# Recurrent memory attention: the chain reduced to its 8 memory rows, x attention in tiles of three segments between its steps

## Chip, cores, metric

One core of one Trainium2 chip. The metric is the time of one execution in device microseconds (us), median of several runs. In the profiles PE is the matrix engine, DVE, ACT and POOL are VectorE, ScalarE and GpSimd, and SP is SyncE, which issues loads and stores; SBUF is the on-chip memory, PSUM that of matmul results.

## The reference, cut to what matters

64 segments of 32 rows of x, one after the other. Each attends over 8 memory rows and its own 32 rows; the 8 memory rows of its output are the memory of the next segment. The kernel computes the output and all gradients (one forward, one backward recurrence). Around it stand a layer norm and a gated feed-forward, which the change hardly touches.

```python
M, seg, H, Dh, Dm = 8, 32, 32, 128, 640      # S = 2048 rows
mem = mem0
for s in range(n_seg):                        # 64 segments
    h = concatenate([mem, xs[s]])             # 40 rows
    q, k, v = (einsum('btd,dhe->bhte', h, W) for W in (Wq, Wk, Wv))
    scores = where(mask, einsum('bhqe,bhke->bhqk', q, k) * scale, -1e9)
    o = einsum('bhqk,bhke->bhqe', softmax(scores), v)
    o = einsum('bhte,hed->btd', o, Wo)
    mem = o[:, :M]                            # the recurrence
    outs.append(o[:, M:])
# result: x + attention * silu(feed_forward(xn)), then the vjp of it all
```

## The kernel before, where the change works

One forward step projects all 40 columns of a segment with the weights as the stationary operand, 128 of them at a time, and adds the x attention of the segment before (`x_attention`, 32 rows by 40) in the same step. The weights stay in SBUF.

```python
def f1_group(hT, qT, kT, h0, nh):
    for (W_, dstp, ceng) in ((Wq, qT, 's'), (Wk_, kT, 'v')):
        pj = ps.tile([P, 12, L], F32, name="pj", tag="pj")          # L = 40
        for hh in range(nh):                                         # hidx = h0 + hh
            for dc in range(DC):                                     # DC = 5
                nc.tensor.matmul(pj[:, hh, :], W_[:, dc, hidx * P:(hidx + 1) * P], hT[:, dc, :], ...)
        k.copy(dstp[:, h0:h0 + nh, :], pj[:, 0:nh, :], eng=ceng)
...
for step in range(T + 1):
    t, tp = step, step - 1
    if t < T:
        ...                                   # load x columns
        v_build(t, hT, vtile)                 # V of memory rows, column-tiled by 4
        for (h0, nh) in hgroups:
            f1_group(hT, qT, kT, h0, nh)      # Q and K of 40 columns
        mem_attention(t, qT, kT, vtile)
    if tp >= 0:
        x_attention(tp, qTs[tp % 2], kTs[tp % 2], vts[tp % 2])
    ...
    for dc in range(DC):                      # output product of 40 columns
        for jc in range(H):
            nc.tensor.matmul(pso[:, dc, :], Wo[:, jc, dc * P:(dc + 1) * P], oTc[:, jc, :], ...)
    ...                                       # next memory, stores
```

The backward recurrence is built the same way (gradients of Q, K, V of 40 rows, three products with transposed weights of 128 columns). The weight gradients follow in a dense stage of their own.

## Time and profile before

| | before |
|---|---|
| median of all runs | 6478.06 us (4 runs, 6474.34 to 6487.07) |
| PE busy | 85% of the span |
| forward recurrence | 1636 us, 25.2 us a step |
| backward recurrence | 2197 us, 34.3 us a step |
| attention weight gradients | 1185 us |

The table by stage and the groups stand in the prediction. The page of the profile cuts the span in 40 slices: the digit is PE's busy share in tenths, and under it the granted clock of PE in tenths of full speed.

```profile
PE   6869999999999579999999999997457878888777
...
PEclk9888888888888679899989899888668989999888
```

In the two recurrences (slices 4 to 13 and 16 to 27) PE is at 9 and the clock mostly at 8 to 9. Over the whole loops it is 0.82 and 0.90.

### The profile page before, as it was taken

The page shows a single profiled execution, that of the slowest core. Times are in us where ns is not written, and L with a number is a line of the kernel's source. Part 1 is how long each engine was busy: PE and PEld are TensorE (multiplying, and loading weights), DVE is VectorE, ACT ScalarE, POOL GpSimd, SP SyncE. Part 2 cuts the span into 40 slices and gives each one's busy share as a digit, 9 for nine tenths or more (in the row PEclk, how much of TensorE's full clock was granted, in tenths as well). Part 3 has the DMA queues.
Part 4 walks back from the last instruction along what each step waited for, and adds up shares of the span by engine and source line. Part 5 has one row for each costly group of instructions (what it writes and reads, how often), then busy time and mean ns, then how long its engine had stood idle before and what let it go on. Part 6 is the DMA issues. An engine that isn't in the chain of part 4 may idle for free.

```text
span 6475.0 us, 255034 instructions
## 1 busy us (share of the span) xinstructions
PE 5517.9 (85%) x117287; PEld 4293.8 (66%) x117490; DVE 2584.9 (40%) x5438; ACT 1820.3 (28%) x3535; POOL 348.9 (5%) x783
## 2 busy tenths in 40 slices
PE   6869999999999579999999999997457878888777
PEld 3426888888888478888888888887123444444344
DVE  5414555555555433344334334333237422222212
ACT  3313444444333222222222222222112022222212
POOL 0000010110011000000000000000000001111110
PEclk9888888888888679899989899888668989999888
DMA  5363333333322652222223223224757655545674
GB/s 178 128 218 101 87 93 91 96 93 89 83 72 70 198 177 83 82 89 84 89 83 90 80 85 89 83 82 79 179 180 192 161 155 196 191 155 171 222 255 165
DMA packets 844915, 824.64 MB, mean 127 GB/s; under 512 B 466240, under 2 KB 652608, under 8 KB 839232
## 3 DMA queue, kind: packets, MB, share of 16 engines
q10 hardware_dynamic: 485568, 399.76, 21.0%
q1 hardware_dynamic: 354496, 387.58, 19.0%
q8 instruction: 918, 15.04, 1.0%
q0 software_dynamic: 3776, 20.97, 0.9%
q14 instruction: 157, 1.29, 0.1%
HBM read 516.86 MB, written 291.22 MB: 125 GB/s over the span
## 4 chain that ended last, share of the span: by engine, by line
PE 65%; DMA 17%; DVE 10%; issue 4%; ACT 3%; ACTq 0%; POOL 0%; another core or an unknown queue 0%; DVEq 0%; SPq 0%; POOLq 0%
PE pgh L949 13%; PE pj L589 6%; PE gacc L1310 5%; PE pso L717 5%; PE pgo L871 4%; PE pgxb L1111 2%; DMA hb_tok<-HB 2%; PE oacc L1336 2%; PE pgot L925 2%; DMA fullxx<-OT 2%; PE pvx L545 2%; PE ptokk L917 2%; PE ptokq L917 1%; PE pv L600 1%; DMA fullx<-GQT 1%
## 5 line engine op out<-in xcount | busy, mean ns | idle before, releaser
L1310 PE MATMUL gacc<-gtok_all,h_all 128*128 128x512 bf16 x2322 | 559.5, 390 | 45.9 <-DVE gwo L92 20.6
L1310 PEld LDWEIGHTS <-h_all 128*128 128x128 bf16 x2400 | 237.1, 100 | 321.2 <-issue 81.5
L949 PE MATMUL pgh<-gQT,WqT 128*128 128x40 bf16 x10240 | 351.1, 183 | 12.7 <-issue 6.3
L949 PE MATMUL pgh<-gKT,WkT 128*128 128x40 bf16 x10240 | 334.6, 182 | 21.8 <-DMA WkT<-WKT 15.7
L717 PE MATMUL pso<-oTc,Wo 128*128 128x40 bf16 x10400 | 344.4, 197 | 5.2 <-issue 1.4
L94 ACT COPY qtok<-ptokq 40x1024 bf16<-40x1024 bf16 x128 | 128.8, 1006 | 768.4 <-PE ptokq L917 768.4
L717 PEld LDWEIGHTS <-Wo 128*128 128x128 bf16 x10400 | 338.8, 108 | 8.2 <-issue 2.6
L949 PE MATMUL pgh<-gVT,WvT 128*128 128x40 bf16 x10240 | 322.0, 182 | 8.9 <-issue 7.9
L949 PEld LDWEIGHTS <-WqT 128*128 128x128 bf16 x10240 | 308.9, 98 | 22.4 <-issue 8.6
L954 DVE CAST goT<-pgh 128x40 bf16<-128x40 f32 x63 | 12.6, 200 | 775.3 <-PE pgh L949 762.1
L949 PEld LDWEIGHTS <-WkT 128*128 128x128 bf16 x10240 | 297.7, 97 | 27.4 <-DMA WkT<-WKT 15.8
L589 PEld LDWEIGHTS <-Wq 128*128 128x128 bf16 x10240 | 275.8, 96 | 46.2 <-issue 45.9
L1279 PE MATMUL pt<-ident,xsrc 128*128 128x128 bf16 x2048 | 172.8, 247 | 152.7 <-DVE xsrc L1268 74.0
L589 PE MATMUL pj<-hT,Wq 128*128 128x40 bf16 x10240 | 290.8, 180 | 14.2 <-ACT qT L94 14.1
L949 PEld LDWEIGHTS <-WvT 128*128 128x128 bf16 x10240 | 292.0, 97 | 11.7 <-issue 10.3
L871 PE MATMUL pgo<-goT,WoT 128*128 128x40 bf16 x10240 | 277.9, 180 | 25.2 <-DMA WoT<-WOT 15.7
L589 PE MATMUL pj<-hT,Wk 128*128 128x40 bf16 x10240 | 290.6, 180 | 2.5 <-issue 2.2
L871 PEld LDWEIGHTS <-WoT 128*128 128x128 bf16 x10240 | 268.1, 96 | 35.1 <-DMA WoT<-WOT 15.8
L1279 PEld LDWEIGHTS <-xsrc 128*128 128x128 bf16 x2048 | 151.1, 112 | 208.9 <-issue 97.5
L589 PEld LDWEIGHTS <-Wk 128*128 128x128 bf16 x10240 | 273.4, 96 | 3.5 <-issue 3.5
L671 POOL TENSOR_TENSOR Px<-ex,rz 32x480 bf16<-32x480 bf16 (+1 forms) x192 | 171.3, 892 | 1460.2 <-DVE rz L670 1125.8
L1271 POOL COPY msrc<-fullx 128x128 bf16<-128x128 bf16 x512 | 152.9, 318 | 1762.3 <-DMA fullx<-GQT 991.0
(255 smaller groups left out, 9652.1 us busy)
## 6 DMA issues: line engine op xcount, KB each, us to landing
fullx<-OT SPq DMA_DIRECT2D x128, 320.0 KB
fullxx<-OT ACTq DMA_DIRECT2D x128, 320.0 KB
fullx<-GQT SPq DMA_DIRECT2D x64, 320.0 KB
fullx<-GQT ACTq DMA_DIRECT2D x64, 320.0 KB
fullx<-GKT SPq DMA_DIRECT2D x64, 320.0 KB
fullx<-GKT ACTq DMA_DIRECT2D x64, 320.0 KB
fullx<-GVT SPq DMA_DIRECT2D x64, 320.0 KB
fullx<-GVT ACTq DMA_DIRECT2D x64, 320.0 KB
```

What stands on the lines that cost most here:

```text
L545: nc.tensor.matmul(pvx[:, :], xnTt[:, dc, :], Wv[:, dc, jn * 512:(jn + 1) * 512], start=(dc == 0), stop=(dc == DC - 1))
L589: nc.tensor.matmul(pj[:, hh, :], W_[:, dc, hidx * P:(hidx + 1) * P], hT[:, dc, :], start=(dc == 0), stop=(dc == DC - 1))
L671: nc.gpsimd.tensor_tensor(Px[:, h0:h0 + nh, :], exv, bc_last(rz[:, 0:nh], L), ALU.mult)
L717: nc.tensor.matmul(pso[:, dc, :], Wo[:, jc, dc * P:(dc + 1) * P], oTc[:, jc, :], start=(jc == 0), stop=(jc == H - 1))
L871: nc.tensor.matmul(pj[:, hh, :], WoT[:, dc, hidx * P:(hidx + 1) * P], goT[:, dc, :], start=(dc == 0), stop=(dc == DC - 1))
L917: nc.tensor.transpose(ptk[:, hh, :], src[:, b8 + hh, :], k.ident[:, :])
L925: nc.tensor.transpose(ptk[:, hh, :], gOT[:, hs + b8 + hh, :], k.ident[:, :])
L949: nc.tensor.matmul(pso[:, dc, :], WT_[:, jc, dc * P:(dc + 1) * P], gX[:, jc, :], start=(i_acc == 0), stop=(i_acc == n_acc - 1))
L1111: nc.tensor.matmul(pgx[:, d0:d0 + dsz], gTt[0:fsz, fc, :], wT[0:fsz, fc, d0:d0 + dsz], start=(i_acc == 0), stop=(i_acc == n_acc - 1))
L1271: nc.gpsimd.tensor_copy(msrc[:, mt2, :, r4, j * M:(j + 1) * M], fulls[j][:, hs:hs + H2, 0:M])
L1279: nc.tensor.transpose(pt8[0:nrow, hh, :], xsrc[:, b8 + hh, 0:nblk, :], k.ident[:])
L1310: nc.tensor.matmul(accs[dc][:, :], h_all[:, kt, dc * P:(dc + 1) * P], gtok[:, kt, jn * 512:(jn + 1) * 512], start=(kt == 0), stop=(kt == N ...
```

## The change

The intent: of the 40 rows of a segment only the 8 memory rows are in the chain from segment to segment. So the chain keeps those alone. Q, K and V of x rows come from dense products ahead of the loop (672 rows) or ride in 24 spare columns of the chain's projection. The projection takes the 32 columns as the stationary operand, in four column tiles of the array at once, and streams the weights. x attention of three segments (24 memory and 96 x rows, a mask between segments) is done in units of 4 heads, as filler between the chain's steps. What one stage hands to another goes through memory. The diff, cut to its core:

```diff
-        def f1_group(hT, qT, kT, h0, nh):
-            ...
-                        nc.tensor.matmul(pj[:, hh, :], W_[:, dc, hidx * P:(hidx + 1) * P], hT[:, dc, :],
+def packed_proj(k, ps, tag, x, W, st, cp):
+    for b in range(2):
+        pj = ps.tile([P, 512], F32, name="pj", tag=tag)
+        for dc in range(k.DC):
+            for g in range(4):
+                c0 = g * 1024 + b * 512
+                nc.tensor.matmul(pj[32 * g:32 * g + 32, :], x[:, dc, :], W[:, dc, c0:c0 + 512],
+                                 ..., tile_position=(0, 32 * g), skip_group_check=True)
+        k.copy(st[:, b * 512:(b + 1) * 512], pj[:], eng=cp[b])
...
-        for step in range(T + 1):
-            ...
+            def xattn(tl, qd):                        # one filler unit: 4 heads of a tile
+                ...                                   # row loads of Q and V on nc.sync
+                pt = ps.tile([P, 4, n], BF16, name="qpt", tag="xt", bufs=1)
+                ...                                   # transposes, copy, mask and scores
+                for j in range(4):
+                    nc.scalar.activation(E[0:n, j, :], sp[:, j, :], ACT.Exp, ...)
+                nc.gpsimd.tensor_tensor(Pb[0:n], E[0:n], bc_last(rz[0:n], n), ALU.mult)
+                nc.gpsimd.dma_start(k.PR[tl][:, h0:h0 + 4, :], Pb[0:n])
+                pp = ps.tile([n, 4, n], BF16, name="xpp", tag="xt", bufs=1)
+                ...                                   # transposes of P, values, store
+            for tl in range(k.NTL + 1):
+                units = []
+                for qd in range(8):
+                    if 0 <= tl - 1:
+                        units.append((xattn, tl - 1, qd))
+                    if tl + 1 < k.NTL:
+                        units.append((kprep, tl + 1, qd))
+                steps = list(range(3 * tl, min(3 * tl + 3, T)))
+                for i, t in enumerate(steps):
+                    with tc.high_priority():
+                        chain(t)
+                    ...                               # a third of the units after each step
...
+    # backward chain: the output gradient goes to memory and comes back by heads
+                nc.sync.dma_start(k.GOS[t].rearrange("r (g c) -> g r c", g=4), sg[:])
+                for a in range(2):
+                    nc.sync.dma_start(gOst[:, a, :], k.GOS[t, 0:8, ...])
...
+    # x gradient, now dense, in the stage of the weight gradients
+                        nc.tensor.matmul(g5[0:nx, :], gT[:, i, j, 0:nx], Ws[i][:, j, 0:512], start=f, stop=l)
+                        nc.tensor.matmul(g1[0:nx, :], gT[:, i, j, 0:nx], Ws[i][:, j, 512:640], start=f, stop=l)
```

## The prediction

> **What bounds the kernel now.** I read first a table of stretches, cut where the first and last instruction of each stage's tiles stand: layer norm and feed-forward forward (to 336), weights and value projection (to 544), the forward recurrence (to 2180), its epilogue, the backward recurrence (2306 to 4503), the feed-forward backward (to 5290), the attention weight gradients.
>
> ```profile
> core 0: us, PE busy (x) PEld busy (x) DVE busy (x) ACT busy (x) POOL busy (x), PEclk, DMA share, GB/s
> 0.00:336.00 336.00, 244.76 (x1499) 131.26 (x1522) 154.61 (x372) 116.92 (x194) 0.84 (x7) 0.91 0.44 151
> 336.00:544.00 208.00, 147.71 (x679) 65.08 (x692) 51.85 (x83) 38.61 (x66) 3.93 (x4) 0.85 0.58 198
> 544.00:2180.00 1636.00, 1560.20 (x46576) 1382.83 (x46572) 892.09 (x1987) 659.02 (x1604) 171.34 (x193) 0.82 0.30 85
> 2180.00:2306.00 126.00, 47.59 (x662) 38.44 (x663) 49.61 (x106) 21.98 (x33) 6.28 (x5) 0.57 1.01 328
> 2306.00:4503.00 2197.00, 2057.47 (x58896) 1911.47 (x58892) 853.35 (x1573) 578.62 (x1006) 13.63 (x63) 0.90 0.29 86
> 4503.00:5290.00 787.00, 516.45 (x2832) 243.27 (x2883) 311.39 (x707) 113.49 (x220) 0.00 (x0) 0.79 0.66 162
> 5290.00:6475.00 1185.00, 943.70 (x6157) 521.46 (x6269) 271.98 (x612) 291.67 (x412) 152.88 (x512) 0.89 0.57 199
> ```
>
> The two recurrences are 3833 of 6475 us, with the PE busy 95% and 94% of them: 25.2 us a step forward (65 steps) and 34.3 us backward (64). They are rows of small matmuls, as the groups say:
>
> ```profile
> L1310 PE MATMUL gacc<-gtok_all,h_all 128*128 128x512 bf16 x2322 | 559.5, 390 | 45.9 <-DVE gwo L92 20.6 <-ACT gtok_all L94 10.7 <-DVE gtok_all L92 5.2
> L949 PE MATMUL pgh<-gQT,WqT 128*128 128x40 bf16 x10240 | 351.1, 183 | 12.7 <-issue 6.3 <-DMA WqT<-WQT 0.5
> L717 PE MATMUL pso<-oTc,Wo 128*128 128x40 bf16 x10400 | 344.4, 197 | 5.2 <-issue 1.4 <-ACT oTc L94 0.5
> ...
> L600 PE MATMUL pv<-Wv,hT 128*8 128x512 bf16 x2560 | 172.7, 383 | 4.4 <-DMA hT<-in_A_mem_dram 4.4
> ```
>
> The mean of one (183 ns) is latency. The pace is start to start in the trace: 25 ns for a 40-column matmul with its own 128-column weights, 56 ns at 128 columns, 216 ns at 512. The pv group is column-tiled in four: its starts come four within 12 ns, then 206 ns later the next four, so four matmuls of 512 cost 216 ns. Full weights thus cost the old kernel almost nothing at 25 ns.
>
> **What the Trainium skill says.** "TensorEngine Tiling (Array Packing)", Performance Considerations, gives each matmul about 60 cycles, so that small ones don't get cheaper; the trace agrees with 25 ns at 8, 32 and 40 columns alike. "TensorE: Matmul & The Clock Gate", Weight-path perf modes, gives fast weight load only to exactly 128 weights; its LDWEIGHTS section has a plain load take columns/1.2 ns. The trace is quicker: 18 ns for 40 columns (Pm), 28 for 64, so columns/2.4; a 120-column weight is then 50 ns, an estimate, against 25 now. The same page, Part 1, says that an idle PE falls to half clock; here the grant is 0.57 in the epilogue and 0.9 in the dense stages. "DMA: Bandwidth & Descriptors", SWDGE vs HWDGE, has GpSimd write the descriptors of its own DMAs; the only four here took 1.03 to 1.72 us of POOL each, and the change issues some 1340 there.
>
> **The change, part by part.** The forward recurrence keeps only the 8 memory rows in its chain; 672 of the x rows are projected densely beforehand, the others ride in 24 spare columns. x attention works in tiles of three segments as filler between chain steps. Gradients of x rows leave the recurrence for a dense stage.
>
> *Before the loop.* 720 matmuls of 512 x 216 ns = 156, 640 transposes at some 75 ns = 48, weights 30: 235 us (now 208). The feed-forward forward takes the 80 transposes of the epilogue: 348.
>
> *One forward chain step*, serially, with about 0.1 us at each handover: Q, K, V as 120 tiled matmuls, 30 x 216 = 6.5, last latency and eviction 1.2; selection 0.35 and copy 0.45; 32 scores on 120-column weights 1.9; copy 0.5, transposes 0.3, maximum and scale 0.7, two exponentials 1.2 (285 to 302 ns for 40 columns now), reciprocal and product 0.65, transposes 0.4, copy 0.45; 32 matmuls on V 1.05; copy 0.45; output, 16 x 136 ns (320 columns) = 2.2 + 0.25; eviction 0.55; six fp32 matmuls, none in this trace, taken at the 0.3 us of the slowest transposes, 1.8; copy 0.25. Sum 21, with filler in the queues 22. So the step falls only from 25.2 to 22: the old projections at 25 ns were good already.
>
> *The filler.* One x-attention unit (4 heads, 8 units per tile of 3 steps) is serial too: scores 0.4, maximum 0.7, scale 0.2, four exponentials 1.7, reciprocal 0.3, POOL product 1.1 (0.98 now), transposes 0.5, copy 0.5, values 0.3, the next unit's K transposes and copy 0.95, Q transposes and copy 1.15: 7.9 us. One PSUM buffer holds both transposes and the K ones, so units don't overlap. The order of the built program shows where they stand: two of three steps have about 1.3 units each, but the first step of a tile has four whole units and a part between Q's selection and its scores, since its K must be ready and the PE runs in order. That is 3.5 + 3 x 7.9 + 6.5 = 34, of which 2 were there anyway: 22 + 32 = 54, or 52 as the filler then is gone. A tile is 2 x 22 + 52 = 96; 21 tiles 2016, the last step 52, a tail of 15 units at 7 = 105: 2173 us, against 1636.
>
> *Output projection*, now its own stage: per tile 32 x (216 + 56 + 42) = 10 us, 22 tiles 220, load 20: 240, against 76.
>
> *Backward.* Weights 35, dense projection of 704 rows 240 x 216 = 52: 87 (now 50). The chain step: projection 10 x 216 with latency and eviction 3.2, selection and copy 0.85, 32 products 1.85, copy and transposes 0.8, softmax gradient 1.2, transposes and copy 0.85, Q gradient 1.5, output 48 x 136 ns = 6.5 + 0.2, eviction 0.55, fold and copy 2: 19.5. Here the order spreads the filler evenly, 2.7 units a step; DVE waits for it add about 1.5: 21. 62 x 21 = 1302, the first steps, which hold some 14 serial units of 5.4, 118: 1420 us, against 2197. A gain of 780.
>
> *Attention weight gradients.* The dense part is new. Per tile and 4 heads: transposes 16 x 54 ns, row gradients 12 x 56 ns, gradient of x 12 x (216 + 56): 4.8 us PE; 8 x 21.5 such are 825, at the 0.8 that the present stage reaches (2400 x 216 + 2560 x 56 ns = 660 of 822 us) 1030. Weight gradients 2640 x 216 = 570 + 30. Output weights 704 x 272 ns = 191, at 0.8 240. Start 10: 1880 us, against 1185.
>
> *Feed-forward backward* loses 80 transposes: 775.
>
> Sum: 348 + 235 + 2173 + 240 + 87 + 1420 + 1880 + 775 = 7158, taken as 7150 us. PE work alone grows: x rows' attention, which lay under the recurrence's weights, is paid again in dense stages.
>
> **Rivals.** (1) The forward filler overlaps after all: if the first step of a tile costs 30 rather than 52, the loop is 1750 and the whole 6700; if also the dense stages run at full pace, 6350. For it: somebody tuned this order; ACT and DVE are at 54% and 40% of the present forward loop. Against: PE order is fixed, and one PSUM buffer ties units together. (2) Faster: chain steps of 18 us both ways and no filler stall give 1300 and 1250 and some 6100. For it: the waits in the backward loop are short now, and the new step has a third of the matmuls. Against: the sums above. (3) Slower: POOL becomes the bound backward, 13 DMAs a step at 1.0 to 1.7 us being 14 to 22 us; or the clock falls to 0.6 in the long filler stretches, where the PE works some 15% of the time: 150 to 300 us, to 7450.
>
> **Range and chances.** Rival 1 and the clock set the range: 6350 to 7700. My sum says slower by 10%, and it takes two errors of its larger terms to come under 6350; but a rebuild of this care is made to win, which I weigh. Faster 0.22, within 2% 0.08, slower 0.70.
>
> **What would show it.** Right: forward steps in a pattern of 22, 22, 52 us; the exponentials and POOL product of x attention on the chain of waits; granted clock under 0.8 forward; about 21 us a step backward; a gradient stage near 1900 us. Wrong: equal forward steps under 25 us; a backward step over 26 with the PE waiting for POOL; a dense stage under 1600.

## The result, and the profile after

| | before | after |
|---|---|---|
| median | 6478.06 us (6474.34 to 6487.07, 4 runs) | 8379.07 us (8372.95 to 8388.02, 4 runs) |
| PE busy | 85% | 72% |
| mean granted clock | 0.86 | 0.79 |

The ratio is 1.294 (95% interval 1.292 to 1.296). Ratios are the mean time of one kernel's fast runs over that of the other's of the same rounds, so not quite the ratio of the medians above. The change makes the kernel slower by 29%; the prediction said 10%.

The stages of after, cut as in the table of before (columns: span, busy time and instructions of each engine, granted clock, DMA share, GB/s):

```profile
core 0: us, PE busy (x) PEld busy (x) DVE busy (x) ACT busy (x) POOL busy (x), PEclk, DMA share, GB/s
0.00:345.00 345.00, 251.25 (x1578) 136.21 (x1602) 161.84 (x393) 125.73 (x210) 3.63 (x25) 0.91 0.54 172
345.00:584.00 239.00, 196.37 (x1360) 129.24 (x1360) 80.87 (x139) 82.76 (x140) 0.00 (x0) 0.90 0.70 246
584.00:3086.00 2502.00, 1630.64 (x21542) 1023.59 (x21543) 642.96 (x1654) 658.02 (x2338) 435.41 (x650) 0.68 0.27 75
3086.00:3313.00 227.00, 226.37 (x2112) 157.39 (x2111) 53.71 (x129) 46.13 (x66) 0.51 (x1) 0.99 0.44 120
3313.00:3415.00 102.00, 58.63 (x240) 25.58 (x244) 18.06 (x29) 13.82 (x24) 0.67 (x3) 0.82 0.77 268
3415.00:5460.00 2045.00, 1397.49 (x24256) 959.06 (x24252) 628.85 (x3184) 315.56 (x784) 675.02 (x1112) 0.71 0.40 109
5460.00:7435.00 1975.00, 1576.96 (x11832) 966.58 (x11832) 484.30 (x1110) 308.72 (x602) 15.76 (x22) 0.94 0.27 76
7435.00:7650.00 215.00, 197.06 (x1408) 107.78 (x1408) 21.19 (x32) 9.49 (x33) 0.00 (x0) 0.95 0.62 133
7650.00:8371.00 721.00, 516.24 (x2739) 240.12 (x2792) 297.86 (x690) 111.90 (x219) 0.00 (x0) 0.80 0.60 165
```

Rows 1 and 2 are the layer norm with the feed-forward and the dense projections; row 3 is the forward loop, row 6 the backward loop, rows 7 and 8 the attention weight gradients. PE is busy 65% of the forward loop and 68% of the backward one, at a clock of 0.68 and 0.71, where the old loops had 95% and 94% at 0.82 and 0.90. The slices of the page show the same:

```profile
PE   7687666666666648576666777758888888787588
...
PEclk9796676666667769776666677789999999997699
```

| stage, us | predicted | measured | difference |
|---|---|---|---|
| layer norm, feed-forward forward | 348 | 345 | -3 |
| weights, dense projections | 235 | 239 | +4 |
| forward loop | 2173 | 2502 | +329 |
| output projection | 240 | 227 | -13 |
| backward weights, dense projection | 87 | 102 | +15 |
| backward loop | 1420 | 2045 | +625 |
| attention weight gradients | 1880 | 2190 | +310 |
| feed-forward backward | 775 | 721 | -54 |
| sum | 7158 | 8371 | +1213 |

So three stages hold the whole miss. What PE waited for in the forward loop (time in total, how often, the longest):

```profile
PE xpp L510 <- POOL xP L506: 378.2, 136, 31.0
...
PE xsp L492 <- ACT qT L486: 77.9, 134, 0.7
PE xpo L515 <- DMA vr<-VS: 77.5, 12, 7.8
...
PE xpo L515 <- DMA vr<-VX: 36.9, 7, 6.8
```

The POOL product of x attention leads, and ahead of it lies a unit's whole softmax; V rows that land late come next. The starts of the first value product of successive chain steps, taken from the trace, are this far apart:

```
us: ... 24.8 24.2 63.0 24.8 24.3 63.8 24.8 24.2 64.6 24.7 24.1 63.3 ...   (predicted 22 22 52)
```

One filler unit inside a 64 us step (start, duration, engine, what, and in brackets the idle time before and who ended it):

```profile
2263.49 0.65 PE L510 MATMUL xpp<-ident,xP 120*120 120x120 bf16 x4 [3.95 <-POOL xP L506]
...
2264.65 0.68 PE L515 MATMUL xpo<-vr,xPT 120*120 120x128 bf16 x4 [0.50 <-DVE xPT L512]
...
2266.10 0.56 PE L484 MATMUL qpt<-ident,qr 120*128 120x120 bf16 x4
...
2267.36 0.66 PE L492 MATMUL xsp<-kT,qT 128*120 128x120 bf16 x4 [0.70 <-ACT qT L486]
...
2270.93 0.98 POOL L506 TENSOR_TENSOR xP<-xE,xrz 120x480 bf16<-120x480 bf16 x1 [4.15 <-issue]
2271.96 0.47 PEld L510 LDWEIGHTS <-xP 120*120 120x120 bf16 x4 [4.13 <-POOL xP L506]
2271.97 0.66 PE L510 MATMUL xpp<-ident,xP 120*120 120x120 bf16 x4 [3.95 <-POOL xP L506]
```

From one `xpp` to the next are 8.48 us, of which PE works some 3.3. Between the scores (2267.36) and the next transposes of P (2271.97) it stands still. The scores of the next unit, which could fill that time, come after those transposes in PE's program. The trace's clock records say that the grant alternates between full and half in stretches of multiples of 3.4 us; in such a 64 us step it is at half for 47.8 us on end, and for 65% of the whole loop.

In the backward loop PE waited for loads:

```profile
PE gvpt L751 <- DMA gvr<-VS: 143.2, 53, 6.8
PE psd L682 <- DMA vTt<-VTD: 130.4, 21, 7.9
PE gkp L775 <- DMA gqx<-QS: 62.6, 16, 7.9
```

These are V rows of the filler, the transposed V of a tile (960 KB, loaded at its start) and Q rows. After a first step of 74 us the steps go 24, 24, 47 us in 13 tiles (in time) and 24, 24, 37 in the last 7. POOL, the third rival of the prediction, is busy 33% of the loop.

### The profile page after: what moved, and what is told of

It reads as the page before. It is cut to its first block, busy times and chain, and to the rows that moved or that the text cites. A ratio compares the mean times of both kernels' runs of the same rounds, so it can differ in the third digit from the quotient of the medians.

```text
span 8371.2 us, 165393 instructions
## 1 busy us (share of the span) xinstructions
PE 6051.0 (72%) x67061; PEld 3745.5 (45%) x67142; DVE 2389.6 (29%) x7360; ACT 1672.1 (20%) x4414; POOL 1131.0 (14%) x1812
## 5 line engine op out<-in xcount | busy, mean ns | idle before, releaser
L882 PE MATMUL g<-w,gT 128*96 128x512 bf16 (+1 forms) x2112 | 640.8, 401 | 0.0
L899 PE MATMUL wg<-gr,hr 120*128 120x512 bf16 (+1 forms) x2640 | 582.0, 379 | 5.2 <-DVE ghacc L888 3.6
L782 POOL DMA_DIRECT2D GXP<-gks x512 | 382.9, 861 | 711.8 <-DVE gks L90 637.4
L883 PE MATMUL g<-w,gT 128*96 128x128 bf16 (+1 forms) x2112 | 477.9, 226 | 0.0
L899 PEld LDWEIGHTS <-hr 120*128 120x128 bf16 (+1 forms) x2640 | 252.7, 98 | 322.8 <-issue 28.6
L882 PEld LDWEIGHTS <-gT 128*96 128x96 bf16 (+1 forms) x2112 | 271.6, 129 | 206.9 <-issue 41.7
L501 ACT ACTIVATE xE<-xsp,xnm 120x120 bf16<-120x120 f32 (+1 forms) x704 | 243.1, 356 | 380.9 <-DVE xnm L497 343.9
L304 PEld LDWEIGHTS <-gkv 128*8 128x8 bf16 x8192 | 226.2, 105 | 200.7 <-DVE gkv L715 39.0
L304 PE MATMUL gpm<-WvT,gkv 128*8 128x320 bf16 x4096 | 263.5, 444 | 32.8 <-DVE gkv L715 32.8
L883 PEld LDWEIGHTS <-gT 128*96 128x96 bf16 (+1 forms) x2112 | 272.4, 129 | 0.0
L304 PE MATMUL pm<-Wo,oTm 128*8 128x320 bf16 x4032 | 248.0, 430 | 4.2 <-DVE oTm L450 1.8
```

Source lines behind the costliest of these rows:

```text
L304: nc.tensor.matmul(pm[p0:p0 + 8, 0:320], x[:, h, :], W[:, h, 320 * b:320 * b + 320], start=(si == 0 and i == 0), stop=(si == last and i == ...
L501: nc.scalar.activation(E[0:n, j, :], sp[:, j, :], ACT.Exp, bias=nmx[0:n, j:j + 1], scale=k.scale, accum_out=Z[0:n, j:j + 1])
L782: nc.gpsimd.dma_start(k.GXP[3 * tl + s, :, :, h0:h0 + 4, :], ks[:, s])
L882: nc.tensor.matmul(g5[0:nx, :], gT[:, i, j, 0:nx], Ws[i][:, j, 0:512], start=f, stop=l)
L883: nc.tensor.matmul(g1[0:nx, :], gT[:, i, j, 0:nx], Ws[i][:, j, 512:640], start=f, stop=l)
L899: nc.tensor.matmul(accs[dc][:], hr[0:n, tl, dc * P:(dc + 1) * P], grs[tl][0:n, i, :], start=(tl == 0), stop=(tl == NTL - 1))
```

## The experiments

Fourteen kernels; single runs unless said, whose state (fast or slow) is not known, so times are given with the loops that the profile shows, and differences under about 30 us of the whole are not read. Kernel before took 6461 to 6493 us beside them.

**Theories.** After the result: (A) PE meets filler units in an order that makes it wait out each one's softmax, and waits for late rows in order too; (B) PSUM and row buffers are too few; (C) the half clock, which follows from PE's pauses; (D) round trips through memory. They are not exclusive; the runs are to size them.

### f_split: filler out of the forward loop

```diff
-                    units.append((xattn, tl - 1, qd))     # in the loop
+def phase3x_xattn(k):                                     # a stage behind it, 3 buffers each
+            for qd in range(8):
+                for tl in range(k.NTL):
+                    xattn(tl, qd)
```

> x attention taken out of the forward loop (only the K transposes stay there) and made a dense stage of 176 units behind it with three buffers each; result correct. Theory 'serial filler': the 64 us steps fall to the 24 us of the others, loop 65 x 24 = 1600 us against 2500; a dense unit costs about 3 us of ACT, 176 x 3 to 4 = 530 to 700; both together 2130 to 2300, the whole 8000 to 8170. Rival 'the chain is slow by itself or the overlap is worth its price': steps fall by less than half of the 40 us, or the dense stage costs over 900, and the whole is 8370 or more.

Measured 9074.55 us: slower by 695. The loop took 1932 us, the steps nearly all 28 to 32 us, not 24; the dense stage 1254 us, 7.1 us a unit at a clock of 0.50. The theory is met only in that the 64 us steps went; what the rival forecast (a dense stage over 900, the whole over 8370) came. The loop's cause is in its waits:

```profile
PE kpt L467 <- DMA kr<-KS: 327.6, 45, 8.7
PE kpt L467 <- DMA kr<-KX: 99.3, 19, 7.1
```

427 us for the rows of the only filler left, the K transposes: a late row of the filler stops the chain. Without these the chain would take (1932 - 427)/64 = 23.5 us a step, an estimate. In the dense stage three buffers changed nothing: the built program still has the scores of a unit behind the values of the one before. So many buffers don't help while the order is serial.

### f_xt2: two PSUM buffers for the filler's transposes

```diff
-                pt = ps.tile([P, 4, n], BF16, name="qpt", tag="xt", bufs=1)
+                pt = ps.tile([P, 4, n], BF16, name="qpt", tag="xt", bufs=2)     # also kpt, xpp
-                psT = ps.tile([n, H, 8], F32, name="psT", tag="ch")
+                psT = ps.tile([n, H, 8], F32, name="psT", tag="c1", bufs=1)     # and the chain's others
```

> Forward loop: the x attention's PSUM transposes get two buffers in place of one (taken from the chain's, which is serial anyway). Theory of the prediction 'one PSUM buffer ties the units': K and Q transposes of the next unit hide under the softmax of this one, 2 to 2.5 us of some 8.8 a unit; the 64 us step falls to about 54, loop 2500 to about 2290. Rival 'the softmax of one unit (maximum, four exponentials, POOL product, transposes) is the serial thing': 64 falls to 60 at most, loop over 2420.

Measured 8279.33 us, the loop 2391 (-111), the long step 57 to 61 us. It lies between the two, nearer to the rival: the buffer was only a part of what tied units together.

### f_pipe and f_pk: the order, then the K rows

f_pipe emits the first half of the next unit ahead of the second half of this one (on top of f_xt2), and gives V rows a second buffer; f_pk gives K rows one too.

```diff
+            def xattn(tl, qd):
+                xattn_a(tl, qd)                 # rows, transposes, scores, softmax
+                if late:
+                    xattn_b(*late.pop())        # transposes of P, values, store: of the unit before
+                late.append((tl, qd))
-                vr = fl.tile([120, 512], BF16, name="vr", tag="vr")
+                vr = fl.tile([120, 512], BF16, name="vr", tag="vr", bufs=2)
-                kr = fl.tile([96, 512], BF16, name="kr", tag="kr")
+                kr = fl.tile([96, 512], BF16, name="kr", tag="kr", bufs=2)      # f_pk only
```

> Forward loop: f_xt2 and, on top, each x-attention unit is emitted in two halves, the first half of the next unit (transposes, scores, softmax) ahead of the second half (transposes of P, values) of this one; V rows get two buffers. The built program now spreads the units over all three steps. Theory 'order': what costs is that PE meets the units one after another, each waiting out its own softmax; steps become even at 28 to 30 us, a tile 113 to 87, loop 2500 to about 1950, whole about 7820. Rival 'engines or buffers under it are slow anyway': a tile stays over 105, the whole over 8200.

Measured 8029.35 us, loop 2153 (another -238), steps 24, 40, 35 in the later tiles, a tile 99. Short of the 1950 expected; its largest wait is again one row load:

```profile
PE kpt L475 <- DMA kr<-KS: 345.6, 47, 10.5
```

> Forward loop: f_pipe and, on top, K rows get a second buffer too (two chain temporaries share buffers to make room). In f_pipe PE still stood 273 us of 1100 before K transposes whose rows came late. Theory 'late loads, PE in order': the steps of 40 and 35 us fall to about 28 and 27, a tile 99 to about 80, loop 2153 to about 1750, whole about 7620. Rival 'the SyncE queue is late anyway': loop stays over 2050.

Measured 7890.22 us, loop 1995 (another -158, not the 400 expected). The K wait went, and the Q rows took its place, with 159 us:

```profile
PE qpt L492 <- DMA qr<-QS: 158.9, 24, 10.1
```

Together the forward loop gives back 507 of its 866 us over the old kernel. A run below, l_bufs, gives V rows their second buffer in the old order: the 114 us of waiting for them go, waits for K rows rise from 33 to 104 us, the long step is 62, and the loop falls by only 24. So most of f_pipe's 238 is the order. But the two buffers, PSUM's 111 and the K rows' 158, come to more: (A) and (B) are both shown, and neither as the larger, since each mend was tried on top of the one before. The rows' lateness is never gone, it moves.

### f_warm: keeping the clock

```diff
+                for i in range(36):
+                    nc.tensor.matmul(pm[:, 384:512], sTm[:, i % 2, :], sTm[:, i % 2, :], ...)
                 mx = ch.tile([P, 2], F32, name="mmx", tag="mmx")
```

> Forward loop: 36 dummy matmuls of 128 columns (2 us) stand in the chain's softmax wait, where PE idles 2.2 us; they write columns that nobody reads, the result stays correct. Theory 'clock': the output projection (4.1 us at half clock) falls to 2.5 and the projections from 9.2 to 7.7, the plain step 24.5 to 21.5, the loop by 150 to 200 us. Rival 'the grant does not come back for so little, or the dummies cost more than they give': loop within 60 us of 2500, or slower.

Measured 8348.9 us, loop 2471 (-31). The output product did what (C) says. Its group, first in after, then in f_warm (busy time, mean ns of one):

```profile
L304 PE MATMUL pm<-Wo,oTm 128*8 128x320 bf16 x4032 | 248.0, 430 | 4.2 <-DVE oTm L450 1.8
```

```profile
L304 PE MATMUL pm<-Wo,oTm 128*8 128x320 bf16 x4032 | 167.4, 324 | 14.7 <-DVE oTm L453 14.6
```

From its first start to its last it falls from 3.59 to 2.35 us a step (mean over 63 steps), against the 2.2 predicted. The projection hardly moved (7.68 to 7.49 us). So 1.24 us a step is won and most of it paid back for the dummies: the wall time follows the rival, the mechanism the theory. The clock in the loop rose from 0.68 to 0.74.

### p6_pipe: the gradient stage in four interleaved pieces

```diff
-            for tl in range(NTL):                # loads, transposes, 3 row gradients, 3 transposes, x gradient
+            s1(0)
+            for tl in range(NTL):
+                if tl + 1 < NTL:
+                    s1(tl + 1)                   # loads, transpose of dS
+                s2(tl)                           # row gradients
+                if tl > 0:
+                    s4(tl - 1)                   # x gradient of the unit before
+                s3(tl)                           # transposes
+            s4(NTL - 1)
```

> Attention weight gradients: a unit (tile and 4 heads) is emitted in four pieces, so that PE meets the transposes of the next unit and the x gradient of the last one between steps that wait for each other. Theory 'handovers': the unit falls from 7.07 us to 4.8 to 5.3 (3.3 us x gradient, 1.5 us others), stage 1975 to about 1640. Rival 'evictions and DMA issues on DVE and ACT bound it': unit stays over 6.3, stage over 1830.

Measured 8055.37 us (-324). From the first row gradient to the last weight gradient 1545 us, after took 1889; a unit takes 5.17 us, within the 4.8 to 5.3 of the theory, which holds. (The run also gives the stage's loads and the transpose of dS three buffers, which the cut leaves out; PE hardly waited for a load in after, so the order and that transpose's buffers are what this shows together.) PE's waits in after:

```profile
PE r6p L867 <- DVE dST L861: 157.6, 159, 1.0
PE r6p L867 <- ACT gr L92: 124.1, 165, 10.2
```

and in p6_pipe, at the same two places:

```profile
PE t6g L885 <- ACT gT L92: 26.0, 137, 1.4
PE r6p L874 <- ACT gr L92: 16.9, 8, 12.2
```

### b_q, b_vsbuf, l_bufs, b_all: four tries on the backward loads

```diff
-                k.load_m(vr, tl, k.VS, c0, c0 + 512, nc.sync)
+                k.load_m(vr, tl, k.VS, c0, c0 + 512, nc.scalar)          # b_q: all of the filler's loads
-                    nc.sync.dma_start(vT[:], k.VTD[tl][:, :, :])
+                    vT = vTs[tl % 2]                                     # b_vsbuf: stays in SBUF
-                vr = fl.tile([120, 512], BF16, name="gvr", tag="gvr")
+                vr = fl.tile([120, 512], BF16, name="gvr", tag="gvr", bufs=2)  # l_bufs, b_all; gqx too
-                vTq = fl.tile([P, 4, n], BF16, name="gvT", tag="gvT")
+                vTq = fl.tile([P, 4, n], BF16, name="gvT", tag="gvT", bufs=2)  # b_all
-                nc.sync.dma_start(k.GOS[t].rearrange("r (g c) -> g r c", g=4), sg[:])
+                ...                              # b_all: rows 0:8 stored first, then 8:32
```

> Backward loop: the loads of the filler units (V rows, output gradient rows, probabilities, Q rows) go from the SyncE queue to the ScalarE queue. Theory 'queue': they come late because SyncE stands still behind the chain's read-backs (140 us on the landing of GOS alone); PE's waits for V rows (143 us) and Q rows (63 us) all but go, loop 2042 to about 1880. Rival 'the transfers themselves are slow, or ScalarE is blocked by them': loop within 40 us of 2042, or slower.

> Backward loop: transposed V of a tile stays in SBUF in two buffers, in place of 176 writes to memory by POOL and a load of 960 KB at each tile's start (some temporaries share buffers to make room). Theory 'tile start': the wait of the scores' gradient for that load (8 us a tile) goes and the row loads behind it come sooner, the 47 us step falls to 36 to 39, loop 2042 to about 1850. Rival 'another wait takes its place' (row loads, GXP): loop over 1970.

> Both loops: the fillers' row loads get a second buffer (V rows forward; V rows and Q rows backward), so a load is issued one unit earlier. Theory 'late loads by single buffers': PE's waits backward for V rows (182 us with PEld) and Q rows (63) shrink by more than half, the 47 us step to about 38, backward loop 2042 to about 1880; forward 64 to 62. Rival 'the transfers are slow however early they start': backward within 50 us of 2042.

> Backward loop: second buffers for V rows, Q rows and transposed V of the filler, and the memory rows of the output gradient are stored ahead of the others, so that their read-back starts sooner. Theory 'each wait hides the next: single buffers and round trips through memory, met in PE order': with the four relaxed together, a tile falls from 96 to about 78, loop 2042 to about 1690. Rival 'the DMA queues cannot deliver this traffic faster': loop over 1900, as with l_bufs alone.

| | whole, us | backward loop, us | backward step, mean of 63, us |
|---|---|---|---|
| after | 8379.07 | 2043 | 31.4 |
| b_q | 8340.81 | 2014 | 31.0 |
| b_vsbuf | 8345.74 | 1999 | 31.3 |
| l_bufs | 8298.53 | 1985 | 30.5 |
| b_all | 8333.55 | 1997 | 30.8 |

(l_bufs's whole has the 24 us of its forward loop in it.) Three rivals won; l_bufs's loop fell by 58 us, just past the 50 of its rival and far from the 160 of its theory. In b_q the wait for V rows fell only from 143 to 128 us and that for Q rows rose from 63 to 121. In the others the waits aimed at shrank or went (but for the gradient rows in b_all: 18 to 82 us), and others took their place. b_vsbuf and b_all also cut the chain's staging tile to one buffer, to make room, and b_vsbuf let other temporaries share; what that cost them is not known. In l_bufs the V rows' wait fell to 33 us, and this came up:

```profile
PE ggpt L765 <- ACT gvT L761: 213.8, 100, 7.4
PE pgkv L721 <- DMA gOst<-GOS: 124.7, 51, 14.4
```

The first is the filler's single buffer of transposed V, whose store to memory must land; b_all doubled it and got waits for gradient rows instead. The second is new to the list and belongs to the chain itself: the output gradient, stored and read back. That b_vsbuf takes away 176 of POOL's DMAs for almost nothing also speaks against POOL as the bound.

### b_nofill, b_nf_gos, b_nf_warm: the backward chain alone

All three are wrong: without the filler its results are zero.

```diff
-                units = [(part1, tl - 1, qd) for qd in range(8)] if tl > 0 else []
+                units = []
+                ...                       # b_nf_gos: 8 memory rows stored in 4 DMAs of their own, the rest by ScalarE
+                for i in range(40):       # b_nf_warm
+                    nc.tensor.matmul(pm[:, 384:512], dw[:, 0:128], dw[:, 128:256], ...)
```

> Wrong on purpose: the backward loop without its filler; what the filler would have written to memory is zero, written before the loop (some 250 us more there). It shows the chain alone. If the prediction's step was mis-sized in the chain itself: 24 us a step as now in the plain ones. If the plain steps of 24 contain waits brought by the filler: 20 to 22. In both cases the 47 us steps are gone but for the wait on the 960 KB load (8 us a tile).

Measured: steps of 24 to 28 us, 26.9 in the mean; from the first scores to the last 1694 us, where after took 1976. So the chain alone is most of the backward loop, and neither of the two expectations was right: alone it is slower than the plain steps of after (24.4). Its waits say why:

```profile
PE pgkv L713 <- DMA gOst<-GOS: 287.1, 96, 6.5
```

4.5 us of each step is PE waiting for the gradient's round trip. In after PE waits only 18 us in all for these rows: the filler's work and waits stand in the same interval. The clock has a part too: the projection at the step's head takes 2.3 us at full clock and 4.0 at half, and it is at full clock in 49 of 64 steps of after, but in only 16 of b_nofill. The wait fits with what l_bufs and b_all showed, where it came up (125 and 82 us) as those went.

> Wrong on purpose, as b_nofill, and the 8 memory rows of the output gradient go to memory in their own small stores, ahead of the 24 others, which ScalarE issues. If the round trip through memory is what the chain waits for: PE's wait for the read-back falls from 4.6 us a step to under 1.5, the step from 27.4 to 23 to 24. If it is the clock: the step stays over 26.

Measured: 25.5 us a step in the mean, 1.4 better. PE's wait for the rows fell from 4.5 to 3.4 us a step only. It is neither expectation: the round trip counts, and it was but little shortened. Part of the gain can be the clock: the projection is now at full clock in 34 of 64 steps.

> Wrong on purpose: b_nf_gos and 40 dummy matmuls of 128 columns (2.2 us) while PE waits for the read-back. If the half clock is the other part: the output product falls from 9.2 to 6.5 us and the projection from 4.0 to 2.5, the step to 3 us or more under that of b_nf_gos, 20 to 21 in all. If not: within 1 us of b_nf_gos.

Measured: 24.8 us a step, and the wait all but gone (23.5 us in the loop, the dummies stand in its place). The output product, in b_nofill and in b_nf_warm:

```profile
L304 PE MATMUL gpm<-WvT,gkv 128*8 128x320 bf16 x4096 | 272.0, 455 | 21.1 <-DVE gkv L715 17.9
```

```profile
L304 PE MATMUL gpm<-WvT,gkv 128*8 128x320 bf16 x4096 | 170.8, 326 | 31.5 <-DVE gkv L722 31.5
```

From first start to last it takes 8.53 us a step in b_nofill, 8.29 in b_nf_gos, 6.77 in b_nf_warm (8.27 in after; 6.5 predicted). As with f_warm the gain on the product is there, 1.5 us, and the wall shows half of it: by the step, the second forecast (within 1 us of b_nf_gos) came. From the first dummy's start to the last one's end are 4.3 us in the mean of the 64 steps. 24.8 less those is 20.5 us, an estimate of the chain with neither cost; the prediction's sum was 19.5.

### best: the mends together

> All mends together: f_pk, b_all and p6_pipe. If the gains add: 8371 - 750 - 350 - 320 = about 6950 us, still 7 per cent slower than the kernel before; it beats it only if forward and backward chains both come under 22 us a step, which nothing so far shows.

f_pk, p6_pipe and b_all in one kernel: 7467.82 us (7461.77 to 7487.04, 4 runs), ratio to before 1.155 (1.153 to 1.157), correct. That is 11% under after and still slower than before. The forward loop took 1989 us and the backward one 1995. The expected 6950 assumed the two loops' mends at sizes that their own runs then did not show.

## Why the prediction was wrong

Direction and reason were right: a sum of small pieces said slower, because the old kernel's 25 ns matmuls were good and the x rows' work comes back in dense stages. The size was wrong by 1213 us, in three stages. Of the prediction's own signs the forward pattern came, and a clock under 0.8 forward (0.68); the backward step and the gradient stage missed theirs, and the backward step passed the 26 us of the signs against it, but with PE waiting for loads and not for POOL. Two slips changed nothing: its table has DVE at 54% and ACT at 40% of the old forward loop, not the other way round, and the terms of its filler unit add to 7.8 us, not 7.9.

- **"One forward chain step ... with filler in the queues 22."** Measured 24.2 to 24.8. The output's term "16 x 136 ns (320 columns) = 2.2" measured 3.59 us, since it runs at half clock behind the softmax's pause, and f_warm brings it to 2.35. The projections, "30 x 216 = 6.5", span 7.68. The third "Rival", "the clock falls to 0.6 in the long filler stretches", saw the clock, but placed it only in those stretches; it is in every step (0.68 over the loop). Some 2.5 us in 43 steps: 107 us.
- **"7.9 us" a unit and "22 + 32 = 54, or 52" for the first step.** The serial pattern was right, and so was its cause in PE's order, as f_pipe shows. The unit measured 8.48 us, at half clock, and the step 64: late V rows (114 us over the loop, some 5 a tile) and the 2.5 us of the chain itself stand in most of the rest, though with the V rows' wait gone (l_bufs) the step is still 62, as K rows come late in their place. Some 11 us in 21 steps: 231 us. "One PSUM buffer holds both transposes ... so units don't overlap" was the lesser part of the cause: doubling it gave 111 us, mending the order and the rows 396 more.
- **Backward: "Sum 19.5 ... DVE waits for it add about 1.5: 21."** This step failed most: 625 us. The chain alone takes 26.9, some 1720 us in all where 64 x 19.5 = 1248 were predicted: by b_nofill 470 of the 625 us are the chain's. The sum left out the round trip of the output gradient (store, landing, read-back: 4.5 us of waiting a step, shown by b_nofill) and priced the output product at 6.5 where half clock makes it 8.5 (shown by b_nf_warm). The filler adds some 325 us to the chain alone (2043 less 1720), against 172 predicted (1420 less 1248). Read inside after, the plain steps are 24.5 in the mean, 147 us over in 42 steps, and the long ones hold the rest; the same time counts in both readings, as the chain's wait hides under the filler's. The claim "the order spreads the filler evenly" was true of PE's order but not of the loads, which bunch at the tile's edge.
- **Dense: "4.8 us PE ... at the 0.8 that the present stage reaches".** A unit measured 7.07 us and not 6.0, because PE waits for two copies in each (158 and 124 us in all); p6_pipe brings it to 5.17 and takes 324 us off, so the term is the handovers. That is 188 of the 310 us. The rest lies at the stage's start (some 50 us for the memory rows, 10 predicted) and at the turns between groups of heads, which no run separates.

The chances were right to lean to slower; the range (6350 to 7700) left out 8379 because it took the clock as one rival among others, and the costs of loads as hidden.

What stays open: why the filler of the backward loop adds its 325 us whatever load is relaxed. The four tries show only that none of these waits holds it by itself. No run takes the chain's round trip out altogether, so what it costs in after is argued from the chain alone. The forward loop's late Q rows in f_pk are open too.

## What to carry to other kernels

When a dense loop is cut down to a short dependent chain, price the chain at the clock that its own pauses will earn it, and price each store that is read back in the same step as a wait. Filler between chain steps is free only if its pieces arrive at the in-order engine with their data landed: emit the first half of the next unit ahead of the second half of this one, and look at which load would be the next to be late. If mends of one wait after another give little, run the chain without its filler; that one run moved the explanation here more than the four before it.

## What the Trainium skill lacked or had wrong

- "TensorE: Matmul & The Clock Gate", Part 1, has the half clock return after an idle window of about 3.4 us. The windows agree (records of 3.4, 6.8, 10.2, 13.7 us, full or half), but it doesn't say how busy a window must be. Here loops in which PE is busy 65% and 68% of the time are at half clock for 65% and 59% of it, and 36 dummy matmuls a step bring the forward share to 53%.
- The same page, LDWEIGHTS: columns/1.2 ns fits this trace at half clock alone. Scores on 120-column weights go at 100 ns each at half clock and 55 at full, products on 128-column weights at 27 ns (half clock), both with 8 columns moving. That fast load is for exactly 128 columns agrees.
- No page has the price of a store that is read back at once: 256 KB stored, then 8 rows of it loaded by two DMAs, take some 10.5 us from the store's issue to the last product on the rows in b_nofill (issued 0.8 us before the first score, SyncE released at 5.0, last product at 9.7), and 4.5 us of PE a step.
- No page has the time of fp32 matmuls this small: six with 8 columns moving show as 12 records and take 1.42 us a forward step in the mean, 0.24 us each; the prediction took 0.3.
